# Chunked attention with memory, then two expert layers, on one core: v loaded by single tokens, and the first loads in another order

## The chip, the core and the metric

The kernel runs on one core of a Trainium2 chip. A core has TensorE (PE in the profile, with its weight loads as PEld), VectorE (DVE), ScalarE (ACT), GpSimd (POOL) and SyncE (SP), each with its own instruction queue, and 16 DMA engines that move data between the device memory and the on-chip memory. DMAs are issued by SP, ACT and POOL. The metric is the device time of one execution in microseconds (us); lower is better.

## What is computed

Three stages in a row. First, attention over 4 batches and 8 heads, 768 tokens a head, 64 columns a token. Each chunk of 32 tokens looks at its own tokens, 16 to the left, 8 to the right, and 8 memory tokens of the head: 64 keys in all.

```
for c in range(nc):                       # 24 chunks a head
    q_c   = q[:, :, c_start:c_end]
    k_full = concat([mem_k, k[:, :, l_start:r_end]])
    v_full = concat([mem_v, v[:, :, l_start:r_end]])
    scores = scale * q_c @ k_full.T
    a = exp(scores - max); a = a / (sum(a) + 1e-9)
    out[:, :, c_start:c_end] = a @ v_full
```

Then x is the result as 3072 rows of 512 columns. Second, a soft mixture of experts: `logits = x @ phi` with 32 slots, a softmax over the rows, `slot_input = d.T @ x`, two matrix products in each of 8 experts (`w1`, relu, `w2`), and a softmax over the slots that combines the slots' results. Third, a layer that only acts on rows with a positive score; the kernel tests for that and branches.

## The kernel before, in words

Everything is float32. Heads go in pairs (h and h + 4), so there are 16 pairs, and each pair is done in two halves of 12 chunks. These 32 halves are the *slots* n of the main loop; the schedule is written out by hand, and each engine takes its instructions in that order.

Buffers. `ktb` holds keys transposed: columns of a head on 64 partitions, for each chunk block a row of keys (`KB` columns with the memory keys at its end). `qTb` holds queries transposed. `vb` are three buffers (`NVH` = 3) for v, used in turn by the slots: 128 partitions, 64 a head, 12 blocks, and a column of ones on either side that gives the softmax's denominator. `kq` are one staging buffer each for k and q: a tile T of 32 blocks is loaded as 128 partitions x 2 x 512 (512 KB), transposed on PE (`transpose_k` L214, `transpose_q` L247), evacuated from PSUM into `ktb` and `qTb`, and the next tile's load is issued on SP right behind (L211). There are 12 tiles, spread over the slots by the table `halves`.

v. `load_v` (L258) brings the 56 tokens of a block in pairs: one partition takes two neighbouring tokens, a row of 512 B, on 28 partitions a head; `load_mem_v` (L285) does the same for the 8 memory tokens on 4 partitions, issued by POOL. `shift_v` (L296) then copies the second token of each pair from partitions 0 to 31 down to 32 to 63 of the head, two POOL copies a slot (L300). The keys stand in the same order, even tokens and odd tokens apart, and so do scores and probabilities. One slot's two loads of v are issued by SP (head x = 0, after the value product of slot n - 1) and by ACT (x = 1, in the next slot, behind its copy of `pts`).

A slot: `scores(n)` on PE (L316); transposes of the probabilities of slot n - 1 (L349) and of x of slot n - 2 (L398); reduction and subtraction on DVE (L329, L333); halves of the next tile's transposes; `shift_v(n)`; `exps` on ACT (L343); the value product of slot n - 1 (L363) and its normalisation (L380 to L382); the loads of v for slot n + 2; and `WPACE` weight pieces of 512 KB issued by ACT (L570). 28 pieces find room in the pool `wa` (`NWA` = 28). After the last slot the rest come from SP and POOL (`NWB` = 15, then as buffers come free), beside the experts' matmuls (L751, L814), and the results go out.

The start (L575 on): k and q of tile 0 and the memory keys `memn` are loaded by SP, POOL fills the constant parts of `vb` (`init_v` L159) and of `ktb`, PE warms up (`warm` L188), `memn` is copied to twice its width by DVE (L589) and transposed (`mem_keys` L194), then k, then q, then the first scores. The loads of v for slots 1 and 2 are issued after these transposes.

Of the kernel before, what the change touches and what calls it, by code (L numbers as in the profile page):

```python
# [18 lines left out]
def kernel(  # L19
# [45 lines left out]
    NWA, NWB, NWG = 28, 15, 3  # L65
# [3 lines left out]
    WPACE = {n: 1 for n in range(28)}  # L69
    WARM = (6, 1, 4)  # L70
# [3 lines left out]
    SUBS = [(0, 0, 16), (16, 20, 12), (28, 16, 4)]  # L74
# [18 lines left out]
    mask = const.tile([P, 4, LC // 2], F32, name="mask")  # L93
# [25 lines left out]
    memkT = keep.tile([P, NU, 2, 2, NM], F32, name="memkT")  # L119
# [38 lines left out]

    def init_v(i, eng):  # L159
        V = vb[i]  # L160
        eng.memset(V[0:64, :, 2 * D + 1:VW], 0.0)
        eng.memset(V[64:P, :, 0:D + 1], 0.0)
        eng.memset(V[0:64, :, 0:1], 1.0)
        eng.memset(V[64:P, :, VW - 1:VW], 1.0)

    def v_cols(V, blk):
        a = V[:, blk, 0:D + 1].unsqueeze(1)
        dims = [list(d) for d in a.ap]
        dims[1] = [2 * D + 1, 2]
        return bass.AP(tensor=a.tensor, offset=a.offset, ap=dims)  # L170


    memn = xp.tile([P, 2, 2, D], F32, tag="x", name="memn")

    def load_mem():
        nc.sync.dma_start(memn[:, :, 0, :], mem_k.rearrange("b h n d -> (b h n) d").rearrange("(f r) d -> r f d", r=P))
# [29 lines left out]
    def load_kq(T, kind):
# [4 lines left out]
        nc.sync.dma_start(kq[kind], src[t * P:(t + 1) * P])  # L211


    def transpose_k(T, x):  # L214
        kp = ps_tp.tile([P, 4, P], F32, tag="tp", name="kp")
        for j in range(4):
            nc.tensor.transpose(kp[:, j, :], kq[0][:, x, j * P:(j + 1) * P], ident)  # L217
        for a in range(2):
            o = ktb[T % 2][64 * x:64 * x + 64, x, a ^ x].rearrange("p m c -> p (m c)")
            o = bass.AP(  # L220
                tensor=o.tensor,
                offset=o.offset + CH // 4,
                ap=[list(o.ap[0]), [KB, TC], [CH // 4 + NM, 2], [4, 2], [1, 4]],
# [4 lines left out]
        if x == 1:  # L228
            load_kq(T + 1, 0)
            new = ktb[T % 2].rearrange("p h a m c -> p (h a) m c")  # L230
            if T % 3:
                old = ktb[(T + 1) % 2].rearrange("p h a m c -> p (h a) m c")
                nc.gpsimd.tensor_copy(new[:, :, 0, 0:8], old[:, :, TC, 0:8])
                nc.gpsimd.tensor_copy(old[:, :, TC, 8:12], new[:, :, 0, 8:12])

            c = 0
            while c < TC:
# [3 lines left out]
                    new[:, :, c:c + n, CH // 2:KB],  # L241
                    memkT[:, u].rearrange("p h a r -> p (h a) r").unsqueeze(2).to_broadcast([P, 4, n, NM]),
# [881 lines left out]
```

## Time and profile before

| | |
|---|---|
| time, median of 3 runs (lowest to highest) | 261.61 us (259.25 to 262.48) |
| time of the profiled execution; its span | 258.95 us; 257.1 us |
| PE, DVE, ACT, POOL busy | 196.4, 123.8, 97.0, 114.9 us |
| moved by DMA | 65.79 MB in 65,478 packets |
| DMA queues: SP's (q1), ACT's (q10), POOL's (q0) | 59.5%, 33.3%, 5.1% of 16 engines' span |

The span runs from the first to the last instruction; the time has a little around it. Busy times of engines overlap, so they don't add up to the span. A DMA share is the time that packets were on their way, divided by the time of 16 engines; where packets of two queues overlap on an engine it can pass 1. Three stages follow each other: the start (to about 17 us, when the first scores run), the 32 slots of attention (to about 185 us), and the experts.

### The profile page before, as it was taken

How to read it: one execution, taken by the hardware profiler on the slowest of the kernel's cores; microseconds unless marked ns; L12 is line 12 of the kernel's file. 1: busy time of each engine (PE TensorE's matmuls, PEld its weight loads, DVE VectorE, ACT ScalarE, POOL GpSimd, SP SyncE). 2: the span in 40 equal slices, each digit the busy share in tenths (PEclk: the TensorE clock that was granted, in tenths of full speed). 3: DMA queues.
4: the chain of work that ended last, by engine and by line, in shares of the span. 5: the costliest groups of instructions: out<-in, count | busy, mean ns of one | idle time of the engine just before them, and what ended most of it. 6: DMA issues, size and time to landing. Idle time of an engine off the chain costs nothing.

```text
span 257.1 us, 7912 instructions
## 1 busy us (share of the span) xinstructions
PE 196.4 (76%) x3166; PEld 145.0 (56%) x3166; DVE 123.8 (48%) x361; ACT 97.0 (38%) x195; POOL 114.9 (45%) x207
## 2 busy tenths in 40 slices
PE   4497889667786877685978687899798999957760
PEld 4486667656565766574766475677573335513620
DVE  4453585345453345466354535747657153122850
ACT  1214647344452464454454534544340021011430
POOL 8916386356665745556575754659610000000000
PEclk9997999999997999999999979999999999999995
DMA  7199999999999999999999999985999999999993
GB/s 208 30 220 236 235 243 225 235 255 251 243 226 244 213 276 260 227 245 240 234 237 256 254 227 226 226 185 136 315 374 352 347 348 348 348 348 368 348 345 100
DMA packets 65478, 65.79 MB, mean 256 GB/s; under 512 B 6950, under 2 KB 50970, under 8 KB 65434
## 3 DMA queue, kind: packets, MB, share of 16 engines
q1 hardware_dynamic: 43106, 41.83, 59.5%
q10 hardware_dynamic: 18824, 20.19, 33.3%
q0 software_dynamic: 3504, 3.19, 5.1%
q8 instruction: 27, 0.44, 0.8%
q14 instruction: 17, 0.14, 0.2%
HBM read 58.86 MB, written 6.29 MB: 253 GB/s over the span
## 4 chain that ended last, share of the span: by engine, by line
DMA 38%; PE 36%; DVE 8%; issue 7%; POOL 4%; ACT 3%; ACTq 0%; SPq 0%; DVEq 0%; POOLq 0%
DMA vb<-in_v_dram 14%; DMA kq<-in_q_dram 13%; PE qp L252 8%; DMA w<-in_moe_w_dram 7%; PE h_ps L751 5%; PE xs L363 5%; POOL vb L300 3%; PE acc L814 3%; DMA vb<-in_mem_v_dram 3%; DMA memn<-in_mem_k_dram 2%; ACT ktb L225 2%; PE sps L462 2%; PE s L316 2%; PE xtp L398 2%; PE o L849 1%
## 5 line engine op out<-in xcount | busy, mean ns | idle before, releaser
L300 POOL COPY vb<-vb 32x768 f32<-32x768 f32 x64 | 53.3, 833 | 52.4 <-DMA vb<-in_v_dram 38.4
L291 POOL DMA_DIRECT2D vb<-in_mem_v_dram x64 | 38.6, 608 | 1.4 <-PE s L316 1.3
L252 PE MATMUL qp<-ident,kq 128*64 128x128 f32 x384 | 30.0, 307 | 11.7 <-DMA kq<-in_q_dram 8.5
L363 PE MATMUL xs<-vb,pts 128*32 128x130 f32 x768 | 30.2, 286 | 11.0 <-issue 5.7
L252 PEld LDWEIGHTS qp<-ident,kq 128*64 128x64 f32 x384 | 24.8, 154 | 16.0 <-issue 13.6
L316 PE MATMUL s<-ktb,qT 128*32 128x128 f32 x768 | 30.4, 283 | 2.0 <-issue 2.0
L363 PEld LDWEIGHTS xs<-vb,pts 128*32 128x32 f32 x768 | 20.3, 111 | 18.7 <-issue 10.4
L380 DVE TENSOR_SCALAR den<-xs 128x6 f32<-128x6 f32 x32 | 5.3, 165 | 51.7 <-PE xs L363 51.5
L351 ACT COPY pts<-pt 128x384 f32<-128x384 f32 x32 | 15.3, 478 | 36.7 <-PE pt L349 33.5
L225 ACT COPY ktb<-kp 64x512 f32<-64x512 f32 x36 | 20.8, 579 | 12.4 <-PE kp L217 6.5
L316 PEld LDWEIGHTS s<-ktb,qT 128*32 128x32 f32 x768 | 23.0, 112 | 4.3 <-issue 2.9
L333 DVE TENSOR_TENSOR pe<-s,mx 128x192 f32<-128x192 f32 (+2 forms) x96 | 22.0, 284 | 4.2 <-PE pt L349 0.3
L254 ACT COPY qT<-qp 128x512 f32<-128x512 f32 x22 | 14.2, 646 | 24.0 <-PE qp L252 24.0
L399 ACT COPY xT<-xtp 128x384 f32<-128x384 f32 x32 | 15.3, 479 | 16.8 <-PE xtp L398 5.2
L349 PE MATMUL pt<-ident,pe 128*128 128x128 f32 x96 | 18.0, 297 | 4.2 <-ACT pe L343 4.0
L398 PE MATMUL xtp<-ident,x 128*128 128x128 f32 x96 | 16.8, 285 | 5.2 <-DVE x L382 2.8
L814 PE MATMUL acc<-w,w 128*32 128x256 f32 x256 | 16.8, 393 | 4.5 <-DMA w<-in_moe_w_dram 4.5
L329 DVE TENSOR_REDUCE mx<-s 128x6 f32<-128x384 f32 x32 | 17.5, 548 | 3.4 <-PE s L316 2.1
L225 DVE COPY ktb<-kp 64x512 f32<-64x512 f32 x12 | 8.3, 695 | 21.0 <-ACT ktb L225 21.0
L382 DVE TENSOR_TENSOR x<-xs,den 128x384 f32<-128x384 f32 x32 | 17.8, 558 | 1.1
L343 ACT ACTIVATE pe<-pe 128x384 f32<-128x384 f32 x32 | 16.7, 523 | 1.9 <-DVE den L380 1.5
L217 PE MATMUL kp<-ident,kq 128*128 128x128 f32 x96 | 14.3, 291 | 2.6 <-DMA kq<-in_k_dram 2.6
(134 smaller groups left out, 253.6 us busy)
## 6 DMA issues: line engine op xcount, KB each, us to landing
w<-in_moe_w_dram SPq DMA_DIRECT2D x33, 512.0 KB
w<-in_moe_w_dram ACTq DMA_DIRECT2D x28, 512.0 KB
kq<-in_k_dram SPq DMA_DIRECT2D x12, 512.0 KB
kq<-in_q_dram SPq DMA_DIRECT2D x12, 512.0 KB
out_dram<-w SPq DMA_DIRECT2D x12, 512.0 KB
vb<-in_v_dram ACTq DMA_DIRECT2D x31, 168.0 KB
vb<-in_v_dram SPq DMA_DIRECT2D x31, 168.0 KB
vb<-in_mem_v_dram POOLq DMA_DIRECT2D x64, 24.0 KB, 7.0
```

Of the source, the lines that this page charges most:

```text
L225: (nc.vector.tensor_copy if x and a else nc.scalar.copy)(o, kp[64 * a:64 * a + 64].rearrange("p j (i o r) -> p i o r j", o=2, r=2))
L252: nc.tensor.matmul(qp[D * x:D * x + D, j, :], kq[1][:, x, c:c + D], ident, start=True, stop=True)
L291: nc.gpsimd.dma_start(vb[n % NVH][p0 + NP:p0 + 32, :, c], mem_v[b, hp + HX * x].rearrange("(r t) d -> r (t d)", t=2).unsqueeze(1).to_broad ...
L300: nc.gpsimd.tensor_copy(V[p0 + 32:p0 + 64, :, c0:c0 + D], V[p0:p0 + 32, :, D + 1:2 * D + 1])
L316: nc.tensor.matmul(o, qT[:, 32 * i:32 * i + 32], KT[:, :, KB * i:KB * i + 32], start=True, stop=not edge)
L329: nc.vector.tensor_reduce(mx, sv.rearrange("p t a c -> p t (a c)"), axis=AX.X, op=ALU.max)
L333: nc.vector.tensor_tensor(out=pv[:, :, :, o:o + w], in0=sv[:, :, :, i:i + w], in1=mx.unsqueeze(2).to_broadcast([P, TH * 2, 2, w]), op=ALU. ...
L349: nc.tensor.transpose(pt[:, t, :], pe[:, 2 * t:2 * t + 2, :].rearrange("p h c -> p (h c)"), ident)
L363: nc.tensor.matmul(xs[32 * g:32 * g + 32, t], pts[:, t, 32 * g:32 * g + 32], v_cols(V, c - HB * z), start=True, stop=True,)
L382: nc.vector.tensor_tensor(out=x[:, TH * z:TH * z + TH].rearrange("p t (h d) -> p t h d", h=2), in0=xs[:, :, 1:2 * D + 1].rearrange("p t (h ...
L398: nc.tensor.transpose(xtp[:, t, :], x[:, TH * z + t, :], ident)
L814: nc.tensor.matmul(acc[32 * j:32 * j + 32, :cw], hM[kf // 4][:, e, kf % 4, :], w_t["w2", e, ci, kf // 4][:, kf % 4, :], start=(e == 0 and ...
```

## The change

v is loaded token by token: a partition takes one token, a row of 256 B, 56 partitions a head and 8 more for the memory tokens, so `shift_v` is gone. `VW` goes from 194 to 136 columns a block, with `VA` = 8 columns between the blocks for the ones. Keys, scores, mask and probabilities stand in the tokens' own order (blocks of 64 keys instead of even and odd halves). q is transposed by the same helper as k (`turned`), half by half, and evacuated by one copy on ACT and one on DVE; before, each half took eight products with 64 columns, and one copy. `mem_keys` makes four products into 64 partitions each, without the doubled `memn`. The freed memory takes two more weight pieces in `wa` (`NWA` 30, `NWB` 13), which slots 26 and 27 issue. The warm-up has 14 matmuls, not 6. At the start ACT issues q, k's transposes come first, and all loads of v and mem_v for slots 0 to 2 are issued ahead of them.

```
-    NWA, NWB, NWG = 28, 15, 3
+    NWA, NWB, NWG = 30, 13, 3
-    WPACE = {n: 1 for n in range(28)}
-    WARM = (6, 1, 4)
+    WPACE = {**{n: 1 for n in range(26)}, 26: 2, 27: 2}
+    WARM = (14, 1, 4)
...
     def mem_keys():
...
-            nc.tensor.transpose(mps[:, f * P:(f + 1) * P], memn[:, f].rearrange("p j d -> p (j d)"), ident)
+            for x in range(2):
+                nc.tensor.matmul(
+                    mps[D * x:D * x + D, f * P:(f + 1) * P], memn[:, f], ident, start=True, stop=True
+                )
...
-        nc.sync.dma_start(kq[kind], src[t * P:(t + 1) * P])
+        (nc.scalar if T == 0 and kind else nc.sync).dma_start(kq[kind], src[t * P:(t + 1) * P])
...
+    def turned(kind, x):
+        tp = ps_tp.tile([P, 4, P], F32, tag="tp", name="qp" if kind else "kp")
+        for j in range(4):
+            nc.tensor.transpose(tp[:, j, :], kq[kind][:, x, j * P:(j + 1) * P], ident)
+        return tp
...
-    def transpose_q(T, a):
-        qp = ps_tp.tile([P, 4, P], F32, tag="tp", name="qp")
-        for j in range(4):
-            c = (2 * j + a) * D
-            for x in range(2):
-                nc.tensor.matmul(qp[D * x:D * x + D, j, :], kq[1][:, x, c:c + D], ident, start=True, stop=True)
-        o = qTb[T % 2].rearrange("p (s j a) -> p s j a", j=4, a=2)
-        (nc.vector.tensor_copy if T == 0 else nc.scalar.copy)(o[:, :, :, a], qp.rearrange("p j s -> p s j"))
-        if a == 1:
+    def transpose_q(T, x):
+        qp = turned(1, x)
+        for a in range(2):
+            o = qTb[T % 2][64 * x:64 * x + 64].rearrange("p (s j a) -> p s j a", j=4, a=2)
+            (nc.vector.tensor_copy if a else nc.scalar.copy)(
+                o[:, :, :, a], qp[64 * a:64 * a + 64].rearrange("p j s -> p s j")
+            )
+        if x == 1:
             load_kq(T + 1, 1)
...
-                ap=[[2 * D, r1 - r0], [CH * D, b1 - b0], [1, 2 * D]],
-            )
-            eng.dma_start(V[p0 + r0:p0 + r1, b0:b1, c], src)
+                ap=[[D, r1 - r0], [CH * D, b1 - b0], [1, D]],
+            )
+            eng.dma_start(V[64 * x + r0:64 * x + r1, b0:b1, D * x:D * x + D], src)
...
-    def shift_v(n):
-        V = vb[n % NVH]
-        for hh in range(2):
-            p0, c0 = 64 * hh, 1 + 2 * D * hh
-            nc.gpsimd.tensor_copy(V[p0 + 32:p0 + 64, :, c0:c0 + D], V[p0:p0 + 32, :, D + 1:2 * D + 1])
...
     load_v(0, 0, nc.sync)
     load_v(0, 1, nc.scalar)
-    nc.vector.tensor_copy(memn[:, :, 1, :], memn[:, :, 0, :])
-    mem_keys()
+    load_mem_v(0)
+    init_kt(1, nc.gpsimd)
+    for i in range(1, NVH):
+        init_v(i, nc.gpsimd)
+        load_v(i, 0, nc.sync)
+        load_v(i, 1, nc.scalar)
+        load_mem_v(i)
     for x in range(2):
         transpose_k(0, x)
-    warm(ps_m, "m", WARM[1])
-    for a in range(2):
-        transpose_q(0, a)
+        if x == 0:
+            mem_keys()
+    for x in range(2):
+        transpose_q(0, x)
     warm(ps_x, "xs", WARM[2])
-    for i in range(1, NVH):
-        load_v(i, 0, nc.sync)
-        load_v(i, 1, nc.scalar)
-    for i in range(NVH):
-        load_mem_v(i)
     load_small()
...
-        shift_v(n)
```

PE's queue from its start to the first scores (`wps` are the warm-up's results, `mps` the memory keys, `kp` and `qp` k and q of the first tile, `s` scores). Before:

```order
L192 MATMUL wps<-ident 128x128 x6
L197 MATMUL mps<-ident,memn 128x128 x2
L217 MATMUL kp<-ident,kq_107 128x128 x8
L192 MATMUL wps<-ident 128x128
L252 MATMUL qp<-ident,kq_108 64x128 x16
L192 MATMUL wps<-ident 128x128 x4
L316 MATMUL s<-ktb_110,qT_109 32x128
```

and now:

```order
L188 MATMUL wps<-ident 128x128 x14
L213 MATMUL kp<-ident,kq_107 128x128 x4
L194 MATMUL mps<-ident,memn 64x128 x4
L213 MATMUL kp<-ident,kq_107 128x128 x4
L213 MATMUL qp<-ident,kq_108 128x128 x8
L188 MATMUL wps<-ident 128x128 x4
L304 MATMUL s<-ktb_110,qT_109 32x128
```

Half of k stands ahead of the memory keys, and q takes 8 matmuls, not 16.

ACT's queue from its start to the first `exps` (`vb_112`, `vb_113`, `vb_111` are the buffers of slots 0, 1 and 2, `kq_108` is q's). Before:

```order
L274 DMA vb_112<-in_v_dram 28x12x128
L225 ACT_TABLE_LOAD
L225 COPY ktb_110<-kp 64x32x2x8 x3
L274 DMA vb_113<-in_v_dram 28x12x128
L274 DMA vb_111<-in_v_dram 28x12x128
L225 COPY ktb_115<-kp 64x32x2x8 x3
L343 ACTIVATE pe<-pe 128x384
```

and now:

```order
L207 DMA kq_108<-in_q_dram 128x2x512
L269 DMA vb_112<-in_v_dram 56x12x64
L269 DMA vb_113<-in_v_dram 56x12x64
L269 DMA vb_111<-in_v_dram 56x12x64
L225 ACT_TABLE_LOAD
L225 COPY ktb_110<-kp 64x32x2x8 x3
L248 COPY qT_109<-qp 64x512 x2
```

q's load and all three loads of v stand ahead of the first copies.

POOL's queue in the slots after the first (`ktb` copies carry edge keys and memory keys, L291 and L285 are the loads of mem_v). Before:

```order
L300 COPY vb_112<-vb_112 32x12x64 x2
L291 DMA vb_113<-in_mem_v_dram 4x12x128 x2
L300 COPY vb_113<-vb_113 32x12x64 x2
L291 DMA vb_111<-in_mem_v_dram 4x12x128 x2
L300 COPY vb_111<-vb_111 32x12x64 x2
```

and now:

```order
L285 DMA vb_113<-in_mem_v_dram 8x12x64 x2
L285 DMA vb_111<-in_mem_v_dram 8x12x64 x2
L285 DMA vb_112<-in_mem_v_dram 8x12x64 x2
```

No copy that needs v stands between the loads of mem_v any more.

## Rows read from the trace of the kernel before

**Rows 1.** Busy time by stretch; last three columns: granted clock, DMA share, GB/s.
```profile
core 0: us, PE busy (x) PEld busy (x) DVE busy (x) ACT busy (x) POOL busy (x), PEclk, DMA share, GB/s
...
7.00:14.00 7.00, 4.10 (x24) 3.85 (x26) 3.66 (x7) 1.74 (x3) 6.30 (x10) 1.00 0.14 32
...
36.00:148.00 112.00, 84.47 (x1610) 69.45 (x1610) 55.59 (x177) 54.28 (x111) 67.56 (x113) 0.94 1.07 241
...
172.00:182.00 10.00, 9.10 (x203) 7.16 (x198) 6.91 (x24) 4.98 (x11) 7.28 (x10) 0.95 0.62 153
196.00:250.00 54.00, 45.87 (x477) 21.29 (x466) 21.89 (x48) 11.12 (x20) 0.00 (x0) 0.95 1.08 351
```

**Rows 2.** Waits from 36 to 176 us: engine, line, releaser; total, times, longest.
```profile
POOL vb L300 <- DMA vb<-in_v_dram: 38.4, 26, 4.3
...
PE qp L252 <- DMA kq<-in_q_dram: 8.0, 5, 3.0
```

**Rows 3.** Timeline of the last slots: start, us, instruction; idle before, releaser.
```profile
174.41 0.89 PE L363 MATMUL xs<-vb,pts 128*32 128x130 f32 x24 [0.17 <-POOL vb L300]
...
177.50 0.89 PE L363 MATMUL xs<-vb,pts 128*32 128x130 f32 x24 [0.33 <-POOL vb L300]
...
180.35 0.89 PE L363 MATMUL xs<-vb,pts 128*32 128x130 f32 x24 [0.25 <-POOL vb L300]
...
182.42 1.81 POOL L300 COPY vb<-vb 32x768 f32<-32x768 f32 x2 [2.13 <-DMA vb<-in_mem_v_dram]
...
184.28 0.89 PE L363 MATMUL xs<-vb,pts 128*32 128x130 f32 x24 [1.33 <-POOL vb L300]
```

**Rows 4.** Packets, MB, share: windows 3:4.5, 178.4:179.2, 5.3:5.9 (two queues), 6.6:7.
```profile
DMA packets 313, 0.61 MB, mean 406 GB/s; under 512 B 16, under 2 KB 16, under 8 KB 313
...
q1 hardware_dynamic: 313, 0.61, 104.5%
...
q10 hardware_dynamic: 271, 0.13, 58.1%
...
q10 hardware_dynamic: 110, 0.05, 73.4%
q1 hardware_dynamic: 114, 0.03, 43.3%
...
q1 hardware_dynamic: 127, 0.06, 92.1%
```

**Rows 5.** Groups by line: count, busy us, mean ns; idle before, releasers.
```profile
L300 POOL COPY vb<-vb 32x768 f32<-32x768 f32 x64 | 53.3, 833 | 52.4 <-DMA vb<-in_v_dram 38.4 <-DMA vb<-in_mem_v_dram 11.2 <-issue 1.0
L291 POOL DMA_DIRECT2D vb<-in_mem_v_dram x64 | 38.6, 608 | 1.4 <-PE s L316 1.3
...
L252 PE MATMUL qp<-ident,kq 128*64 128x128 f32 x384 | 30.0, 307 | 11.7 <-DMA kq<-in_q_dram 8.5 <-issue 3.3
...
L225 ACT COPY ktb<-kp 64x512 f32<-64x512 f32 x36 | 20.8, 579 | 12.4 <-PE kp L217 6.5 <-DMA vb<-in_v_dram 5.4
...
L217 PE MATMUL kp<-ident,kq 128*128 128x128 f32 x96 | 14.3, 291 | 2.6 <-DMA kq<-in_k_dram 2.6
...
L225 DVE COPY ktb<-kp 64x512 f32<-64x512 f32 x12 | 8.3, 695 | 21.0 <-ACT ktb L225 21.0
```

**Rows 6.** Timeline of the start: start, us, engine, line, operation; idle before, releaser.
```profile
1.37 2.93 PE L192 MATMUL wps<-ident 128*128 128x128 f32 x12 [1.37 <-POOL ident masks.py:199]
...
7.56 2.24 DVE L589 COPY memn<-memn 128x128 f32<-128x128 f32 x1 [3.44 <-DMA memn<-in_mem_k_dram]
...
10.36 1.91 PE L217 MATMUL kp<-ident,kq 128*128 128x128 f32 x8
...
12.68 3.33 PE L252 MATMUL qp<-ident,kq 128*64 128x128 f32 x32
...
15.93 1.16 PE L192 MATMUL wps<-ident 128*128 128x128 f32 x8
17.02 0.43 PE L316 MATMUL s<-ktb,qT 128*32 128x128 f32 x8
```

More of the change, by code (lines that the diff above doesn't have):

```diff
@@ L92 @@
     onesrow = const.tile([P, CH], F32, name="onesrow")
-    mask = const.tile([P, 4, LC // 2], F32, name="mask")
+    mask = const.tile([P, 2, LC], F32, name="mask")
     quad = const.tile([P, 4], F32, name="quad")
@@ L118 @@
     ssum = keep.tile([P, 1], F32, name="ssum")
-    memkT = keep.tile([P, NU, 2, 2, NM], F32, name="memkT")
+    memkT = keep.tile([P, NU, 2, NMEM], F32, name="memkT")
     wpools = ctx.enter_context(ExitStack())
@@ L155, in init_kt, with v_view @@
         eng.memset(ktb[i], 0.0)
+    def v_view(n, off):
+        return vb[n % NVH][:, off:off + HB * VW].rearrange("p (b c) -> p b c", c=VW)
     def init_v(i, eng):
[L160 to L173, printed above, removed]
+        eng.memset(v_view(i, VA)[0:64, :, D:2 * D + 1], 0.0)
+        eng.memset(v_view(i, 0)[64:P, :, VA - 1:VA + D], 0.0)
+        eng.memset(v_view(i, 0)[0:64, :, VA - 1:VA], 1.0)
+        eng.memset(v_view(i, VA)[64:P, :, 2 * D:2 * D + 1], 1.0)
+    memn = xp.tile([P, 2, D], F32, tag="x", name="memn")
     def load_mem():
-        nc.sync.dma_start(memn[:, :, 0, :], mem_k.rearrange("b h n d -> (b h n) d").rearrange("(f r) d -> r f d", r=P))
+        nc.sync.dma_start(memn, mem_k.rearrange("b h n d -> (b h n) d").rearrange("(f r) d -> r f d", r=P))
     def load_small():
@@ L278, in load_v @@
             lo = 1
-            rows(LC // 2, NP, 0, 1)
+            tokens(LC, NP, 0, 1)
         if bh == B * H - 1 and z == 1:
             hi = HB - 1
-            rows(0, NP - RC // 2, hi, HB)
-        rows(0, NP, lo, hi)
+            tokens(0, NP - RC, hi, HB)
+        tokens(0, NP, lo, hi)
     def load_mem_v(n):
@@ L306, in scores @@
     def scores(n):
-        s = ps_s.tile([P, TH, 4, 32], F32, tag="s", name="s")
+        s = ps_s.tile([P, TH, 2, 64], F32, tag="s", name="s")
         for t in range(TH):
@@ L316, in scores @@
                 nc.tensor.matmul(
-                    o, qT[:, 32 * i:32 * i + 32], KT[:, :, KB * i:KB * i + 32], start=True, stop=not edge
+                    o, qT[:, 32 * i:32 * i + 32], KT[:, :, KB * i:KB * i + 64], start=True, stop=not edge
                 )
                 if edge:
-                    m0, m1 = (0, LC // 2) if c == 0 else (32 - RC // 2, 32)
+                    m0, m1 = (0, LC) if c == 0 else (64 - RC, 64)
                     nc.tensor.matmul(
```

77 lines of the change are left out of this document (32 added, 45 removed).

## The prediction

> **What bounds the kernel now.** I read the busy times by stretch first [rows 1], because one share for the whole span mixes three different stages. Look at the last two columns of each row. From 36 to 148 us, in the slots of attention, the 16 DMA engines have a share of 1.07, and yet move 241 GB/s. From 196 to 250 us the share is the same (1.08), but 351 GB/s move. So in both stretches a packet is always on its way on every engine, and what differs is what a packet brings. PE is busy 84.47 of 112 us between 36 and 148. The slots thus run at the pace of the DMA engines; PE has 27.5 us to spare there, DVE and ACT half their time. Two rows show gaps: a share of 0.14 from 7 to 14 us, after the first loads (6.0 us of empty engines), and 0.62 from 172 to 182 us, in the last slots.
>
> Then I asked who waits [rows 2]. Leave out the engines that wait for PE: in the slots POOL's shift of tokens waits 38.4 us for v, and PE's transposes wait 8.0 us for q. Both name transfers. A check: the last slots load neither q, k nor weights, and they follow each other at 174.41, 177.50 and 180.35 us [rows 3], every 2.8 to 3.1 us, while all 32, from the first scores at 17.02 us to the last product at 184.28, take 5.2 us each. What costs 2 us a slot is traffic.
>
> So I look at what a packet costs [rows 4]. Rows of 2 KB alone: 313 packets take 104.5% of 16 engines in 1.5 us; without the 16 that are under 512 B that is 84 ns each. Rows of v (512 B) alone: 271 packets, 58.1% of 0.8 us, 27.4 ns each. A line through the two has 8.4 ns at zero bytes and 0.037 ns a byte. In a crowd everything is dearer: v's rows beside those of mem_k take 64 ns (110 packets, 73.4% of 0.6 us), and one half of v by itself can also take 46 ns (127 packets, 92.1% of 0.4 us).
>
> **The change, part by part.** *v in single tokens.* A slot has 28 x 12 x 2 = 672 packets of 512 B now and 1,344 of 256 B afterwards, with the same bytes. By the line a row of 256 B takes 17.9 ns, so a pair takes 35.8 instead of 27.4: 8.4 ns more. The crowded row agrees: the 256-byte rows of mem_k took 36.5 ns (114 packets, 43.3%) beside v's 64 [rows 4], a pair thus 73, 9 more. From below the price is nothing, if a crowd is limited by bytes and the 8.4 ns vanish in waiting. From above it is 27 ns, if a pair costs 73 where a row of v now takes 46. I take 8.4, to which both measured pairs are nearest. 32 slots carry 21,504 packets; the first three slots' loads go into time that is empty now and the last three stand outside the saturated stretch, so 26 slots count: 17,472 x 8.4 ns / 16 engines / 1.06 (the share at which they are full) = 8.7 us, or 1.03 us for each ns. The cover, where there is one, is those two gaps; without it the six slots would add 2.0 us.
>
> One page of the Trainium skill speaks against this edit: "DMA: Bandwidth & Descriptors", section "Specifications", gives 512 B as the least transfer for full rate and says that the engines read, modify and write below it. This case's trace does not bear it out: mem_k's rows of 256 B took 0.57 of v's beside them.
>
> *The shift goes.* POOL loses 64 copies, 53.3 us [rows 5]. In the saturated slots this buys nothing: the wait of POOL for v becomes a wait of PE for the same v. At the end it does: the last four value products each waited for the shift, 0.17, 0.33, 0.25 and 1.33 us [rows 3], 2.1 us together, and POOL's 2 x 0.83 us of shift and 2 x 0.61 us of issue are as long as such a slot. I take 2.0 us off. If mem_v's transfer is late there in place of the shift (POOL waited 2.13 us for it before the last shift), 0.3 us remain lost and the gain is 1.7. Issuing mem_v takes 608 ns for 48 rows [rows 5], so for 96 rows between that and twice as much; POOL, rid of 1.7 us a slot, hides either.
>
> *q transposed as k is.* 384 recorded matmuls become 96: 30.0 us become about 96 x 291 ns, as k's take, or with their overlap k's 14.3 us [rows 5]. PE saves 15.7 us, hidden behind the DMA except at the start. The evacuation turns from two copies a tile over 128 partitions, on ACT but for the first tile, into two on ACT and two on DVE over 64. Priced as k's copies of the same size, 579 ns on ACT and 695 ns on DVE [rows 5], DVE gets 22 x 0.7 = 15 us more, in slots where it is half idle, and ACT no more than before. Without that cover 0.7 us per copy would show. The new layout of keys, mask and score subtractions changes strides and not numbers of elements; I price it at nothing for the same reason, between no change and a copy's own length.
>
> *The start.* Now PE's transposes of k stand behind those of mem_k, which wait for the copy of memn (7.56 to 9.80 us) [rows 6]. They begin at 10.36 us and the first scores at 17.02. Afterwards k comes first in PE's order and the copy is gone. q is issued by ACT beside k; both are 1.05 MB, at 406 GB/s [rows 4] 2.6 us, so landed by about 5. The longer warm-up is 14 matmuls, 28 recorded: at the pace of the first ones (2.93 us for 12) they end at 8.2 us, at the pace of the later ones (1.16 us for 8) at 5.4 [rows 6]. Say k's transposes begin at 7. To the first scores it was 6.7 us, of which 3.33 for q; now 8 transposes (1.1 to 1.9 us) and four products for mem_k between (about as much) stand there: 5 to 6 us. The first scores come near 12.5, 4.5 us earlier. The loads of v for slots 1 and 2, which followed k's copies on ACT, are issued ahead of them and fill the gap of 6.0 us. The gain lies between 3.5 (slow warm-up) and 6.0 (all of the gap); I take 5.0. What is late next is k and q of the second tile, behind more v traffic; that is in the 8.7.
>
> *Two more weight pieces in the slots, two fewer after.* The tail is saturated: 1.05 MB at 351 GB/s [rows 1] are 3.0 us off. In the slots they meet the gap of 172 to 182 us, 10 x (1.07 - 0.62) / 1.07 = 4.2 us wide, which covers most: I take 2.5 off. Without that cover they cost 1.05 MB / 241 GB/s = 4.4 us and the edit loses 1.4.
>
> Sum against the profiled execution (span 257.1, time 258.95 us): 258.95 + 8.7 - 2.0 - 5.0 - 2.5 = 258.1, so 258 us. That execution is 1.0% under the median of the three runs, 261.61; a median after may stand as much higher. What a measurement of this kernel tells from no change is about 2%, 5.2 us.
>
> **Rivals.** *Small rows are nearly free.* If a crowd is limited by bytes, the price falls to 0 to 3 ns: 258.95 - 9.5 + 0 to 3.1 = 249.5 to 252.5 us. For it: one half of v takes 46 ns a row at times and 27.4 at others, so much of the time is waiting and not handling. Against it: both pairs of [rows 4] show 8 to 9 ns more.
>
> *Small rows are dear.* If the price is 15 ns or more, T = 258.95 - 9.5 + 15.5 = 265 us; at 27 ns it is 277. It ends slower from 14.3 ns on (9.5 + 5.2 us over 1.03). For it: the row of 46 ns against a pair of 73. Against it: those two are from different moments.
>
> *A row of 256 B costs as much as one of 512.* Each engine would then need 27.4 ns more a pair: 28 us, T = 278 us. This is what reading, modifying and writing below 512 B could do; the row of 0.57 speaks against it. The rule is that of the skill's page named above.
>
> *The slots wait for the chain, not for traffic.* Then q's 15.7 us on PE alone would come off beside the 9.5, T = 234 us, and the shift's 1.7 us a slot would be more. The shares of [rows 1] speak against it.
>
> **How the numbers follow.** My forecast has a chance of 0.46 with a range of its own of 253 to 263; nearly free rows 0.28, dear rows 0.18, as costly as 512 B 0.03, the chain 0.05. Faster by over 2%: 0.28 + 0.05 and 0.02 of the forecast's lower edge, 0.35. Slower: 0.18 + 0.03 and 0.01 of its upper edge, 0.22. The rest, 0.43, is within 2%. The range must leave out no more than 2 in 10: from 249 (nearly free rows) to 269 (dear rows up to 19 ns).
>
> **What would show it.** The profile after should have about 87,000 packets, twice v's; a pair of 256 B at 35 to 40 ns alone; first scores near 12.5 us; no empty stretch between 7 and 14 us; POOL at some 60 us busy; and between 36 and 148 us a share still near 1.07 at some 225 GB/s, with slots of about 5.5 us. If the rate there stays at 240 GB/s, the rows were free; if it falls under 215, they were dear. If DMA shares fall well under 1 in the slots, my reading of the bound was wrong.

## The result, and the profile after

The changed kernel takes 251.52 us (median of 4 runs, 249.67 to 252.84), the kernel before 261.25 in the same series (259.25 to 262.48): a ratio of 0.963, 95% interval 0.9534 to 0.9726. It is faster by 3.7%. The forecast of 258.0 (no difference that can be measured) was not the case that came; the rival "small rows are nearly free" (249.5 to 252.5 us) gives the right time, and as the runs below show, for the wrong reason. The medians here and below are over all runs of a kernel, slow ones too; without these the ratios on record change by at most 0.018.

Busy time of the changed kernel by stretch, the same four as in [rows 1] (last three columns: granted clock, DMA share, GB/s):

```profile
core 0: us, PE busy (x) PEld busy (x) DVE busy (x) ACT busy (x) POOL busy (x), PEclk, DMA share, GB/s
7.00:14.00 7.00, 5.21 (x62) 3.94 (x60) 3.60 (x7) 3.07 (x5) 5.74 (x13) 1.00 1.15 220
36.00:148.00 112.00, 83.23 (x1551) 66.65 (x1549) 68.42 (x204) 61.79 (x121) 33.75 (x74) 0.97 1.10 254
172.00:182.00 10.00, 6.46 (x66) 5.70 (x63) 3.03 (x11) 1.69 (x4) 0.00 (x0) 0.66 0.83 263
196.00:250.00 54.00, 39.43 (x418) 20.17 (x410) 19.69 (x42) 10.62 (x19) 0.00 (x0) 0.90 0.92 300
```

The gap of 7 to 14 us is gone (share 1.15 for 0.14). In the slots the engines are as full as before (1.10 for 1.07) but move 254 GB/s for 241, with twice as many rows of v. The tail (the experts' stretch behind the slots), 351 GB/s at 1.08 before, has lost: 300 at 0.92. And from 172 to 182 us TensorE's granted clock is 0.66, where it was 0.95.

Four moments cut the span into stages. From the timelines of DVE (row maxima of the 3rd and of the 28th slot) and of PE (value products of the last slot), and of POOL:

```profile
21.77 0.55 DVE L317 TENSOR_REDUCE mx<-s 128x6 f32<-128x384 f32 x1
...
149.06 0.55 DVE L317 TENSOR_REDUCE mx<-s 128x6 f32<-128x384 f32 x1
...
166.33 0.88 PE L349 MATMUL xs<-vb,pts 128*32 128x130 f32 x24 [2.42 <-DMA vb<-in_v_dram]
169.59 1.51 PE L349 MATMUL xs<-vb,pts 128*32 128x130 f32 x24
176.10 1.53 PE L349 MATMUL xs<-vb,pts 128*32 128x130 f32 x24 [3.27 <-DMA vb<-in_v_dram]
...
163.57 2.23 POOL L556 DMA_DIRECT2D w<-in_moe_w_dram  x3
```

In the kernel before, the last value products start at 184.28 us [rows 3], and the row maxima and POOL's last loads stand here:

```profile
27.33 0.55 DVE L329 TENSOR_REDUCE mx<-s 128x6 f32<-128x384 f32 x1
...
164.57 0.54 DVE L329 TENSOR_REDUCE mx<-s 128x6 f32<-128x384 f32 x1
...
184.18 2.16 POOL L570 DMA_DIRECT2D w<-in_moe_w_dram  x3
```

| Stage of the profiled execution, us | Before | After | Predicted | Measured |
|---|---|---|---|---|
| start to the 3rd row maximum | 27.3 | 21.8 | -5.0 | -5.6 |
| 3rd to 28th row maximum (25 slots) | 137.2 | 127.3 | +8.7 | -9.9 |
| to the last value products | 19.7 | 27.0 | -1.5 | +7.3 |
| to the end of the span | 72.8 | 74.9 | -3.0 | +2.1 |
| span | 257.1 | 251.0 | -0.8 | -6.1 |

(The two pieces' -2.5 is split as it was worked out, 0.5 in the slots and -3.0 behind them; the profiled execution after is the slowest of its four, that of before lies under all others of its own, so the medians are further apart.) One stage came as predicted. The slots are 18.6 us better than the sum, and the two last stages 13.9 worse. (The marks of the 25 slots don't hold quite the same traffic: 33.13 MB lie between them before and 32.25 after, so some 3.5 us of the 9.9, at 253 GB/s, are bytes that moved out of the stage.) At the end of the slots the last value products now wait 3.27 us for v instead of 1.33 for the shift. Two things stand beside the last loads of v that did not before: the two weight pieces of slots 26 and 27, and POOL's three weight loads, which stood behind the shift until 184.18 us and are now issued at 163.57. The runs below tell more of the first than of the second.

### The profile page after: what moved, and what is told of

It reads as the page before. It is cut to its first block, busy times and chain, and to the rows that moved or that the text cites. A ratio compares the mean times of both kernels' runs of the same rounds, so it can differ in the third digit from the quotient of the medians.

```text
span 251.0 us, 7227 instructions
## 1 busy us (share of the span) xinstructions
PE 186.2 (74%) x2898; PEld 135.6 (54%) x2898; DVE 134.2 (53%) x380; ACT 103.2 (41%) x197; POOL 61.1 (24%) x142
## 2 busy tenths in 40 slices
DMA packets 85691, 65.73 MB, mean 262 GB/s; under 512 B 48914, under 2 KB 70930, under 8 KB 85650
## 4 chain that ended last, share of the span: by engine, by line
DMA 42%; PE 32%; DVE 10%; ACT 7%; issue 3%; ACTq 1%; POOL 0%; SPq 0%; DVEq 0%; POOLq 0%
DMA vb<-in_v_dram 26%; DMA kq<-in_q_dram 11%; PE h_ps L734 5%; PE acc L797 4%; ACT ktb L225 4%; PE wps L188 4%; DMA out_dram<-w 3%; PE qp L213 3%; PE xtp L384 2%; PE xs L349 2%; DMA kq<-in_k_dram 2%; DVE qT L248 2%; PE sps L448 2%; PE o L832 2%; DVE x L368 2%
## 5 line engine op out<-in xcount | busy, mean ns | idle before, releaser
L285 POOL DMA_DIRECT2D vb<-in_mem_v_dram x64 | 37.2, 585 | 61.8 <-PE xs L349 54.8
L349 PEld LDWEIGHTS xs<-vb,pts 128*32 128x32 f32 x768 | 21.2, 114 | 18.6 <-issue 12.1
L225 ACT COPY ktb<-kp 64x512 f32<-64x512 f32 x36 | 23.1, 642 | 8.3 <-PE kp L213 7.9
L304 PEld LDWEIGHTS s<-ktb,qT 128*32 128x32 f32 x768 | 21.8, 111 | 7.6 <-issue 5.4
L384 PE MATMUL xtp<-ident,x 128*128 128x128 f32 x96 | 17.2, 290 | 11.5 <-DVE x L368 8.7
L336 PE MATMUL pt<-ident,pe 128*128 128x128 f32 x96 | 17.9, 296 | 8.0 <-ACT pe L330 7.8
L248 DVE COPY qT<-qp 64x512 f32<-64x512 f32 x24 | 17.0, 707 | 12.1 <-ACT qT L248 11.8
L213 PE MATMUL qp<-ident,kq 128*128 128x128 f32 x96 | 15.1, 289 | 6.9 <-DMA kq<-in_q_dram 6.0
L384 PEld LDWEIGHTS xtp<-ident,x 128*128 128x128 f32 x96 | 10.9, 146 | 16.3 <-PE pt L336 14.0
L248 ACT COPY qT<-qp 64x512 f32<-64x512 f32 x24 | 17.0, 710 | 6.4 <-PE qp L213 6.0
L368 DVE TENSOR_TENSOR x<-xs,den 128x384 f32<-128x384 f32 x32 | 17.8, 558 | 1.1
L797 PE MATMUL acc<-w,w 128*32 128x256 f32 x256 | 15.7, 382 | 1.8 <-DMA w<-in_moe_w_dram 1.8
L336 PEld LDWEIGHTS pt<-ident,pe 128*128 128x128 f32 x96 | 10.1, 143 | 12.8 <-ACT pe L330 10.6
L213 PEld LDWEIGHTS qp<-ident,kq 128*128 128x128 f32 x96 | 11.4, 147 | 9.1 <-issue 7.1
```

Of the source, the lines that this page charges most:

```text
L213: nc.tensor.transpose(tp[:, j, :], kq[kind][:, x, j * P:(j + 1) * P], ident)
L225: (nc.vector.tensor_copy if x and a else nc.scalar.copy)(o, kp[64 * a:64 * a + 64].rearrange("p j (i o r) -> p i o r j", o=2, r=2))
L248: (nc.vector.tensor_copy if a else nc.scalar.copy)(o[:, :, :, a], qp[64 * a:64 * a + 64].rearrange("p j s -> p s j"))
L285: nc.gpsimd.dma_start(v_view(n, VA)[64 * x + NP:64 * x + 64, :, D * x:D * x + D], mem_v[b, hp + HX * x].unsqueeze(1).to_broadcast([NMEM, H ...
L304: nc.tensor.matmul(o, qT[:, 32 * i:32 * i + 32], KT[:, :, KB * i:KB * i + 64], start=True, stop=not edge)
L336: nc.tensor.transpose(pt[:, t, :], pe[:, 2 * t:2 * t + 2, :].rearrange("p h c -> p (h c)"), ident)
```

## The experiments

Edits are shown shortened, as are views; the whole edit of a run can be longer. Rates are those of 36 to 136 us, which all kernels spend in the slots. For comparison, the kernel before and the changed one over these 100 us:

```profile
36.00:136.00 100.00, 75.76 (x1450) 62.29 (x1450) 49.98 (x159) 48.18 (x100) 60.31 (x100) 0.93 1.07 239
```

```profile
36.00:136.00 100.00, 73.06 (x1360) 58.56 (x1359) 60.15 (x179) 54.05 (x105) 29.98 (x63) 0.97 1.10 255
```

"25 slots" is the stage from the 3rd to the 28th row maximum of the profiled execution. The runs came in five series, so each has the kernel before of its own series beside it; its median lies between 261.25 and 264.95 us, its runs scatter by several us within a series, so a difference of less than 2% between two series says little.

| Run | v's rows | Partitions a half | Rows start at | Median, us | Before, us | Ratio | GB/s | 25 slots, us |
|---|---|---|---|---|---|---|---|---|
| before | 512 B | 28 | 4 to 28 B past 32 B | | 261.25 | 1 | 239 | 137.2 |
| after | 256 B | 56 | 32 B | 251.52 | 261.25 | 0.963 | 255 | 127.3 |
| e1c_two_dmas | 512 B, twice the DMAs | 28 | 4 to 28 B past | 269.35 | 262.31 | 1.027 | 223 | 149.1 |
| e1_small_rows | 256 B, twice the DMAs | 28 | 4 to 28 B past | 280.70 | 262.31 | 1.070 | 215 | 156.6 |
| e2_shift_back | 256 B | 56 | 32 B | 248.66 | 262.31 | 0.948 | 253 | 129.3 |
| e5_q_thrice | 256 B | 56 | 32 B | 249.87 | 262.31 | 0.953 | | |
| e6_before_aligned | 512 B | 28 | 32 B | 258.03 | 264.95 | 0.974 | 248 | 134.1 |
| e7_unaligned | 256 B | 56 | 4 B past 32 B | 258.90 | 264.95 | 0.977 | 243 | 132.1 |
| e3_pieces_back | 256 B | 56 | 32 B | 244.49 | 264.95 | 0.923 | 255 | 128.5 |
| e8_va64 | 256 B | 56 | 256 B | 229.20 | 264.95 | 0.865 | 288 | 114.8 |
| e9_all_lines | 256 B; k, q, weights too | 56 | 256 B | 220.86 | 263.59 | 0.838 | 293 | 111.3 |
| e10_before_lines | 512 B | 28 | 256 B | 250.02 | 263.59 | 0.949 | 266 | 125.2 |
| e11_28_partitions | 256 B | 28 | 32 B | 264.06 | 263.59 | 1.002 | 231 | 140.5 |
| e12_late_pieces | as e9 | 56 | 256 B | 226.11 | 263.80 | 0.857 | 289 | 112.6 |

### The price of a small row by itself

e1_small_rows, and e1c_two_dmas as its control:

```diff
 # kernel before, load_v
-    eng.dma_start(V[p0 + r0:p0 + r1, b0:b1, c], src)          # rows of 2 tokens
+    for j in range(2):                                        # rows of 1 token
+        eng.dma_start(V[p0 + r0:p0 + r1, b0:b1, cj:cj + D], src_j)
 # control: two DMAs of 6 blocks each, rows of 2 tokens
+    for i0, i1 in ((b0, HB // 2), (HB // 2, b1)):
+        part(r0, r1, i0, i1)
```

> The kernel before, with each load of v cut into two DMAs whose rows are 256 B (one token each), still on 28 partitions a head and with the shift kept. Only the rows' size, their number (43,008 in place of 21,504) and the number of DMAs change. Theory of the prediction's sum (a pair costs 8.4 ns more, 1.03 us a ns): about 261.3 + 8.7 = 270 us. Rival A (a crowd is limited by bytes, rows nearly free): 260 to 264 us, with the rate between 36 and 148 us still near 241 GB/s. Rival B (a pair at 27 ns more): 285 us or more. Rival C (the rows of 256 B are themselves what made the changed kernel's slots faster): under 257 us and a rate near 254 GB/s.

> Control of the run above: the kernel before, with each load of v cut into two DMAs of six blocks each, rows still 512 B. If the number of DMAs and their issue cost nothing: 260 to 263 us. If two more issues a slot on SP and ACT delay something, they add up to 64 times an issue's 0.1 to 0.6 us, so 265 us or more, and the run above has to be read against this one and not against the kernel before.

Stretch of the slots, first e1_small_rows, then the control:

```profile
36.00:136.00 100.00, 73.18 (x1316) 59.59 (x1307) 43.59 (x139) 40.96 (x87) 52.25 (x87) 0.90 1.10 215
```

```profile
36.00:136.00 100.00, 74.99 (x1376) 62.27 (x1374) 45.44 (x147) 43.30 (x91) 55.98 (x92) 0.91 1.04 223
```

The control was not free: twice the DMAs for the same rows cost 7 us in the median and 12 in the 25 slots of the profile. So only the difference of the two counts: halved rows cost 7.4 us in 25 slots, 11.4 in the medians. With 16,800 pairs there, 7.4 us x 16 engines x 1.06 / 16,800 are 7.5 ns a pair. The prediction's 8.4 ns and 8.7 us were right for what they named, and "nearly free" is refuted. Something else of the change must have gained about 17 us in the slots.

### Neither the shift nor PE

e2_shift_back and e5_q_thrice:

```diff
 # changed kernel, ahead of exps(n)
+    for hh in range(2):
+        nc.gpsimd.tensor_copy(r, r)     # 32 x 768 of v, each half
 # changed kernel, turned()
+    for _ in range(3 if kind else 1):
         nc.tensor.transpose(tp[:, j, :], kq[kind][:, x, j * P:(j + 1) * P], ident)
```

> The changed kernel, with the two POOL copies a slot put back where the shift stood (32 partitions x 768 of v, copied onto themselves; the value products wait for them, and the memory's loads stand behind them on POOL). Theory of the prediction (in saturated slots the shift is hidden; it shows only at the end): 251.5 + 2, so 252 to 254.5 us, and slots 3 to 27 as long as in the changed kernel, 121 us. Rival (the slots wait for a chain in which v's landing, the shift and the value products follow each other, and the free buffer for the next v comes later by it): most of the 9 us that slots 3 to 27 became shorter come back, 258 to 261 us, and the rate between 36 and 148 us falls from 254 towards 241 GB/s.

> The changed kernel, with each transpose of q done three times over (the last one counts), so that PE has 192 more transposes of some 290 ns, 28 to 30 us recorded and about twice the 15 us that the change took off PE for q. Theory of the prediction (PE's time is hidden behind the DMA in the slots): 251.5 to 253 us. Rival (the slots wait for a chain on PE, so q's saving made them faster): 9 us or more are added, 260 us or above; at 4 to 6 us added the truth lies between, and PE's part of the gain in slots 3 to 27 is about half of what is added.

Neither is slower than the changed kernel: 248.66 and 249.87 us. The slots are paced neither by POOL nor by PE, as predicted. (The profiled execution of e5_q_thrice took 258.39 us, far from its median, so only its times are read.) That the shift put back does not slow the kernel but seems to make it 2.9 us faster (1.1%, in another series) was foreseen by neither theory. Its timeline of POOL and PE at the end:

```profile
172.98 1.71 POOL L622 COPY vb<-vb 32x768 f32<-32x768 f32 x2 [0.93 <-DMA vb<-in_mem_v_dram]
174.63 2.23 POOL L556 DMA_DIRECT2D w<-in_moe_w_dram  x3
...
174.74 0.89 PE L349 MATMUL xs<-vb,pts 128*32 128x130 f32 x24
```

POOL's weight loads are held back again until 174.63, the last value products wait for nothing, and they stand 22.8 us behind the 28th row maximum, not 27.0. The shift had been a brake on these loads. That their early issue is what cost the time is likely, not shown: no run moves these loads by themselves, and in e3_pieces_back below they are issued as early (163.10 us) without harm of that size.

### Where v's rows begin

The block of v in the buffer was 194 words wide with v one word in, and is 136 wide with v eight words in. The buffers begin at multiples of 32 B. A block of 194 words is 8 B longer than a multiple of 32 B, so v's rows stood 4, 12, 20 or 28 B behind one; now all stand on one. The prediction did not price this. e6_before_aligned gives that to the kernel before, e7_unaligned takes it from the changed one:

```diff
 # e6: kernel before
-    VW = 3 * D + 2                      # v at word 1 of a block
+    VW = 3 * D + 8                      # v at word 8
 # e7: changed kernel
-    VA = 8
-    VW = 2 * D + VA
+    VA = 9
+    VW = 2 * D + 8
```

> The kernel before, with one difference of layout: each block of v in the buffer is 200 words wide in place of 194, and v's rows begin at a multiple of 32 B in place of 4 B behind one. Rows stay 512 B, on 28 partitions a head, with the shift; one weight piece moves from the slots to the tail for the room (1 to 1.5 us by the prediction's rates). New theory (the changed kernel also brought v's rows to multiples of 32 B, and that, not the size of the rows, is what made the slots faster): the slots lose the 9 us that the changed kernel gained there and the 8 to 11 us that the smaller rows cost beside, so 242 to 252 us, with over 254 GB/s between 36 and 148 us. Rival (alignment is nothing; the spread over 56 partitions did it): 261 to 264 us and 241 GB/s.

> The changed kernel with v's rows one word further on: each begins 4 B behind a multiple of 32 B, as in the kernel before; blocks keep their width, rows their 256 B and 56 partitions. New theory (alignment): the slots become as slow as those of the run with small rows in the layout of before, which had 215 GB/s between 36 and 148 us: 251.5 + 15 to 20, so 265 to 272 us. Rival (the spread over 56 partitions, or something else of the change, made the slots faster): 250 to 253 us and 254 GB/s.

e7_unaligned in the slots:

```profile
36.00:136.00 100.00, 73.69 (x1319) 59.88 (x1323) 59.08 (x175) 51.88 (x101) 29.19 (x62) 0.93 1.12 243
```

Both theories miss. Alignment is worth 4.8 us of slots in the changed kernel (243 against 255 GB/s) and 3.2 in the kernel before (248 against 239), by one profile each: a part of the gain and not all of it. (The medians of e6_before_aligned and of before are not clear of their spread: 254.8 to 262.5 us against 261.1 to 267.4.) (The first scores of e7_unaligned also come 5.4 us later, since ACT waits 11.8 us for POOL's clearing of the buffers, so the stretch is read here and not the median.) Packets of a moment in which one queue alone loads v, for e7_unaligned:

```profile
DMA packets 444, 0.11 MB, mean 227 GB/s; under 512 B 444, under 2 KB 444, under 8 KB 444
q1 hardware_dynamic: 444, 0.11, 97.7%
```

0.5 us x 16 engines x 0.977 / 444 = 17.6 ns a row: the line of [rows 4] gave 17.9. So an unaligned row need not cost more. But two queues with nothing but such rows are crowd enough: from 6.25 to 6.75 us of the same trace 366 rows have a share of 1.216, 26.6 ns each, and 182 GB/s move. In e8_va64 below, whose rows begin at multiples of 256 B, a moment with two queues (7.0 to 7.5 us) has 501 rows at 1.116, 17.8 ns each, and 251 GB/s.

### How many partitions

e11_28_partitions loads the changed kernel's rows onto half as many partitions:

```diff
 # changed kernel with the pieces of before, load_v: 28 partitions x 24 rows in place of 56 x 12
-    ap=[[D, NP], [CH * D, b1 - b0], [1, D]]
+    ap=[[D, NP // 2], [CH // 2 * D, 2 * (b1 - b0)], [1, D]]
```

> The run with the weight pieces put back (244.5 us), with each half of v loaded onto 28 partitions in place of 56, in as many rows of 256 B at multiples of 32 B and as many DMAs; half of each window's tokens are not loaded, and others stand in their place, so only the time is read. Theory of the spread (28 partitions take the same bytes more slowly): between 36 and 136 us the rate falls from 255 to about 240 GB/s, and the time rises to 250 to 258 us. Rival (the spread is nothing): 253 to 257 GB/s and 244 to 247 us; the clearing of whole buffers at the start may add up to 2 us in either case.

```profile
36.00:136.00 100.00, 76.43 (x1288) 61.37 (x1288) 56.39 (x167) 48.60 (x97) 28.73 (x61) 0.86 1.11 231
```

231 GB/s against 255, 12.1 us more in the 25 slots: the theory of the spread holds, and more strongly than it said. All traffic got slower, not only v: on the mean of the 25 slots a row of 256 B took 27.1 ns in place of 24.9, and a row of 2 KB (k, q, weights) 127.8 in place of 117.7. (Another 7.7 us lie ahead of the first row maximum, where the buffers are cleared. The profiled execution took 266.39 us, 2.3 more than the median; one of the ten took 892.83.) What the run does not separate: its rows also come from tokens 16 apart in place of 32. That 28 partitions are slower does not hang on that alone, as the next pair shows.

### Rows on whole lines of 256 B

e8_va64 puts v's rows of the changed kernel at multiples of 256 B, e10_before_lines those of the kernel before:

```diff
 # e8: changed kernel with the pieces of before
-    VA = 8
-    VW = 2 * D + VA
+    VA = 16                             # 64 B behind the buffer's start: a multiple of 256 B
+    VW = 2 * D + 64                     # 768 B
 # e10: kernel before
-    VW = 3 * D + 2
+    VW = 4 * D                          # 1 KB, v at word 16
```

> The changed kernel with v's rows brought from multiples of 32 B to multiples of 256 B (blocks of 192 words in place of 136), and, for the room, 28 weight pieces in the slots as before; so it is read against the run with the pieces put back. If 32 B is all that counts: the same as that run within 1.5 us. If a row of 256 B that begins inside a 256-byte line costs a second access: 4 to 10 us faster than that run, so 241 to 250 us, and more than 254 GB/s between 36 and 148 us.

> The kernel before, with v's rows of 512 B brought to multiples of 256 B (blocks of 256 words in place of 194; still 28 partitions a head, with the shift and the order of start of before). For the room, 25 weight pieces in the slots and 18 behind them. If lines are what counts, a row of 512 B pays 2 in place of 3, so the slots gain at least as much as the changed kernel's did by the same step (255 to 288 GB/s between 36 and 136 us): 280 GB/s or more against the 239 of before, and 240 to 248 us. If larger rows are still cheaper than pairs of small ones by the prediction's 8.4 ns, over 295 GB/s there. If the 28 partitions hold it back, it stays under 265 GB/s and above 250 us.

e8_va64 in the slots and in the tail, then e10_before_lines in the slots:

```profile
36.00:136.00 100.00, 80.05 (x1545) 64.78 (x1534) 69.12 (x207) 60.03 (x120) 34.74 (x76) 0.98 1.07 288
160.00:190.00 30.00, 28.74 (x362) 13.14 (x364) 12.70 (x33) 4.36 (x10) 0.00 (x0) 1.00 1.10 349
```

```profile
36.00:136.00 100.00, 80.34 (x1603) 66.20 (x1598) 52.90 (x173) 53.05 (x109) 64.95 (x108) 1.00 1.07 266
```

This is the largest single effect of the study: 229.2 us against the 244.49 of e3_pieces_back, 13.7 us of it in the 25 slots. All rows of 256 B took 24.6 ns on the mean of e3_pieces_back's trace and 19.1 here. They are not the whole gain: in the 25 slots their time on the way, divided by 16 engines, fell by 10.3 us (51.3 to 41.0), and that of the rows of 2 KB, whose own start had not moved, by 8.4 us (81.2 to 72.8; 117.7 to 104.2 ns a row). The sum is more than 13.7 because the share fell too, from 1.10 to 1.06. So v's rows off the line also held up the rows beside them. e10_before_lines gains too (266 against 239), but is nearest to its third case: rows of 512 B on 28 partitions stay slower than rows of 256 B on 56 (288). These two kernels also differ in the shift and the start; and v's own rows are not what is left between them, since a row of 512 B takes 36.8 ns there and a pair of 256 B 38.2 here, while the rows of 2 KB take 117.4 and 104.7.

The Trainium skill, page "DMA: Bandwidth & Descriptors", section "How a descriptor splits into AXI transactions", says of reading that an access must start at a multiple of 256 B, so that a descriptor (one row here) which starts behind one fetches the bytes from that multiple on, and counts accesses in steps of 32 B. In the device memory all of v's rows start at a multiple of 256 B from the tensor's start; what the runs move is their start in the on-chip memory, of which the section does not speak. If its count held there too, an estimate by it is: a row of 256 B takes 8 steps on the line and 9 to 15 off it, 11.5 on the mean where the rows of a buffer start in turn at all multiples of 32 B, and 12.6 where they start 4 B behind these. That is 30% less from 32 B to 256 B and 10% more from 32 B to 4 B behind; the traces show 22% less (24.6 to 19.1 ns) and 10% more (24.6 to 27.0 ns in e7_unaligned). The count thus fits in its order and roughly in size; that it is the mechanism no run shows.

### Weights, k and q on whole lines: a faster kernel

```diff
 # e9: e8, with 128 B of padding ahead of the tiles of k, q and the weights
+    keep.tile([P, 32], F32, name="pad")
-    VA = 16
+    VA = 48                             # v stays at a multiple of 256 B
```

> The run with v's rows at multiples of 256 B (28 weight pieces in the slots), and k's, q's and the weights' tiles, whose rows of 2 KB and 1 KB began 128 B behind such a multiple, shifted to one as well (128 B of padding ahead of them). If a row pays for every 256-byte line it touches: rows of 2 KB pay 8 in place of 9 and rows of 1 KB 4 in place of 5, the slots move over 300 GB/s in place of 288, and the time is 4 to 12 us less than that run's 229.2 us, 217 to 225. If only v's short rows were hurt, because they are many: 228 to 230 us. The stretch after the slots, at 349 GB/s with a share of 1.10, tells apart whether rows of 1 KB are bound by handling (then it goes faster) or by something outside the engines (then it stays at 349).

e9_all_lines in the same two stretches:

```profile
36.00:136.00 100.00, 81.84 (x1635) 66.37 (x1630) 72.32 (x215) 60.97 (x122) 36.12 (x78) 1.00 1.07 293
160.00:190.00 30.00, 29.16 (x344) 12.31 (x344) 11.50 (x26) 3.95 (x8) 0.00 (x0) 1.00 1.09 384
```

220.86 us (217.25 to 224.90), 0.838 of the kernel before (13 runs, 257.0 to 268.6): the fastest of the study, 8.3 us under e8_va64 by one line of padding. The 28th row maximum comes at 131.7 us, so the first row holds 4 us of the sparser stretch behind it. The tail, rows of 1 KB that had begun 128 B off, goes from 349 to 384 GB/s at the same share: it was bound by the handling of its rows. By the same count of the Trainium skill, carried over in the same way, such a row pays 36 steps for 32; the rates, 1.10 apart, agree roughly.

### The two weight pieces

e3_pieces_back undoes them; e12_late_pieces moves four pieces of e9 into its last slots, whose engines stand partly empty:

```diff
 # e3: changed kernel
-    NWA, NWB, NWG = 30, 13, 3           # and two pieces each in slots 26 and 27
+    NWA, NWB, NWG = 28, 15, 3
 # e12: e9
-    WPACE = {n: 1 for n in range(28)}
+    WPACE = {n: 1 for n in range(4, 32)}
```

> The changed kernel with 28 weight pieces in the slots and 15 behind them, as before. Prediction's theory (two pieces moved are worth 2.5 us): 251.5 + 2.5 = 254 us. Rival (in the changed kernel the two extra pieces, which stand in the 27th and 28th slot, crowd out the last loads of v, so what the tail gains the last slots lose): 249 to 251.5 us, with the last value products nearer to the 28th softmax than the 28.1 us of the changed kernel.

> The fastest run so far (v's rows, and k's, q's and the weights', at multiples of 256 B; 220.9 us), with its 28 weight pieces issued in slots 4 to 31 in place of 0 to 27. In that run the share of the DMA engines is 0.75 from 136 to 148 us, some 3.6 us of empty engines, because the last four slots carry no piece. Theory 1 (pieces are harmless wherever engines are empty): four pieces, 2.1 MB, leave slots 0 to 27 at 293 GB/s, 7.1 us less there, and take 5.5 us at 382 GB/s in the last slots, 3.6 of them in the gap: 215 to 218 us. Theory 2 (as in the changed kernel, weights issued beside the last loads of v make these late, and the tail cannot start before the last value product frees the room): the last value products come 5 us or more later behind the 28th softmax than the 19.2 us there, and the time is 221 to 226 us.

Last value products in the timeline of e3_pieces_back, with the first product of the experts, then of e12_late_pieces:

```profile
170.19 0.89 PE L349 MATMUL xs<-vb,pts 128*32 128x130 f32 x24 [1.03 <-DMA vb<-in_v_dram]
...
180.31 8.93 PE L734 MATMUL h_ps<-w,sinM 128*32 128x512 f32 x80 [0.45 <-DVE sinM L714]
```

```profile
156.59 1.52 PE L350 MATMUL xs<-vb,pts 128*32 128x130 f32 x24 [5.90 <-DMA vb<-in_v_dram]
```

The two pieces cost the changed kernel 7 us instead of gaining 2.5: without them it takes 244.49 us, and its last value products stand 19.1 us behind the 28th row maximum, not 27.0. In e12_late_pieces the four pieces fill the empty share (0.75 to 0.94 from 136 to 148 us), and the kernel is 5.2 us slower than e9, since the last products wait 5.90 us for v. So the rival of the first run and theory 2 of the second hold, the first by more than it said (244.5 us for 249 to 251.5): the tail begins when the last products free the buffers, so what is loaded beside the last rows of v is paid in full.

The wait also costs on PE. Stretch of 170 to 180 us and first product of the experts in the changed kernel, then the same stretch of e3_pieces_back:

```profile
170.00:180.00 10.00, 6.46 (x80) 5.02 (x70) 3.69 (x12) 2.09 (x5) 0.00 (x0) 0.67 0.82 247
188.75 6.78 PE L734 MATMUL h_ps<-w,sinM 128*32 128x512 f32 x60 [0.45 <-DVE sinM L714]
```

```profile
170.00:180.00 10.00, 9.11 (x145) 7.73 (x145) 5.58 (x22) 3.07 (x8) 0.89 (x13) 1.00 1.08 357
```

While PE stands waiting for v, its granted clock falls to the lower of its two levels, 1.2 GHz (0.50 from 168 to 171 us, behind a wait of 2.42 us, and from 175 to 181, in and behind that of 3.27); in e3_pieces_back it stays at 1.00. The last products take 1.53 us in place of 0.89, and the experts' first product comes 12.7 us behind them in place of 10.1. Of the 8.4 us by which it comes later than in e3_pieces_back, 2.5 lie in that stretch.

## Why the prediction was right in its range and wrong in its case

- *What bounds the kernel.* Right: with the shift back or PE's work for q trebled the time does not rise, and every change of what a row costs moves it.
- *v in single tokens, +8.7 us.* The term is right (7.4 us by itself), the edit was not read to its end: it also doubles the partitions a load covers and moves the rows' start, which the prediction put at nothing without a word. From the pairs of runs: +7.4 (halved rows) - 12.1 (56 partitions for 28) - 4.8 (32 B) = -9.5 us, against the -9.9 of the table. Each of the three is shown; that they add up so well is luck. They come from different layouts and one profile each, the -9.9 holds some 3.5 us of bytes that left the stage, and by rates the same pairs would make 239 x 215/223 x 255/231 x 255/243 = 267 GB/s, where the changed kernel has 255. "If the rate stays at 240 GB/s, the rows were free" was a bad test: it rose to 254, and the rows were not free.
- *A row of 256 B as dear as one of 512.* Halved rows cost 7.5 ns a pair by themselves, far from this rival's 27.4. The Trainium skill, page "DMA: Bandwidth & Descriptors", section "Specifications", names reading, modifying and writing below 512 B; the doubling that this rival took from it is not borne out. That such rows move fewer bytes in the same time is borne out (35.2 ns for a pair alone, 27.4 for one row of 512 B).
- *The shift, -2.0.* Too large: without the two pieces (e3_pieces_back) the last stage of the slots takes 19.1 us in place of the 19.7 of before, 0.6 less. The shift had also held POOL's weight loads back. "What is late next" was asked of mem_v's transfer, not of the loads queued behind the shift on POOL.
- *q and the evacuation.* Right: both are hidden. Groups of the changed kernel by line:

```profile
L248 DVE COPY qT<-qp 64x512 f32<-64x512 f32 x24 | 17.0, 707 | 12.1 <-ACT qT L248 11.8
...
L213 PE MATMUL qp<-ident,kq 128*128 128x128 f32 x96 | 15.1, 289 | 6.9 <-DMA kq<-in_q_dram 6.0 <-DVE ktb L225 0.7 <-ACT ktb L225 0.2
```

  PE's 30.0 us [rows 5] became 15.1 (15.7 saved were forecast, 14.9 came), and DVE has 17.0 us of copies of q, less the first tile's of before (15 forecast).
- *The start, -5.0.* Right: -5.6 to the 3rd row maximum. The timeline of its start, against [rows 6]:

```profile
7.32 0.60 PE L213 MATMUL kp<-ident,kq 128*128 128x128 f32 x4
...
13.01 0.44 PE L304 MATMUL s<-ktb,qT 128*32 128x128 f32 x8 [0.84 <-DVE qT L248]
```

  k's transposes begin at 7.32 us and the first scores at 13.01 (7 and 12.5 forecast).
- *The page's counts.* 85,691 packets for 87,000, POOL 61.1 us busy for 60, a pair of rows alone 35.2 ns (twice the 17.6 of e7_unaligned) for 35 to 40: right.
- *The two pieces, -2.5.* Wrong in sign: they cost 7 us. The gap of 172 to 182 us [rows 1] was read as room. It is the time in which the last loads of v have the engines to themselves, and the tail waits for them.
- *What would show it.* Some 225 GB/s and slots of 5.5 us were expected between 36 and 148 us; 254 GB/s and 5.1 us came. This sign said that the account of the slots was wrong, whatever the time.

The errors have opposite signs (-18.6 in the slots, +13.9 behind them). That the range held the time is luck.

## To carry to other kernels

Before a transfer is costed by the size of its rows, look at where its rows begin in the buffer and over how many partitions it spreads: here blocks of 768 B and 128 B of padding took 24 us off a kernel of 244, more than any reordering. A gap in the DMA share beside the last loads that a stage waits for is not free room. When an instruction is removed, ask what was queued behind it that now starts sooner, and beside what.

## What the runs showed of the hardware that was not expected

- A row that is off a line cost nothing more in a moment with one queue (17.6 ns for 256 B, 4 B off), half as much again with two queues of such rows (26.6 ns against 17.8 on the line), and some 30 to 40% in the mixed traffic (24.6 to 27.0 ns on the mean of all rows of 256 B, 19.1 on the line). The rows of 2 KB beside them got slower too (116.3 ns on the mean of e3_pieces_back's trace, 104.7 of e8_va64's).
- 350 GB/s in the tail was no limit of the memory: 384 with rows on the line.
- Twice the DMAs for the same rows cost 12 us in 25 slots, 0.24 us for each DMA more. Why, no run tells.
- 28 partitions take the same rows more slowly than 56 (231 GB/s against 255). The number of engines is not the reason: each further DMA of e1c_two_dmas brings 14 completions, and the changed kernel's loads have 14 too. What the reason is stays open.
- In e12_late_pieces slots 0 to 3 carry no piece (share 0.67 from 14 to 36 us for 0.98 in e9), and the 11th row maximum comes at 54.3 us as in e9 (54.4). With all rows on the line the first slots are no longer paced by traffic; by what they are, was not tried.
